# First MLP of a fused attention and two-MLP kernel: the second layer follows the first at a distance of four steps

## The chip, the cores and the metric

The kernel runs on one core of a Trainium2 chip. The metric is the device time of one execution in microseconds; of the kernel before there are three runs, with a median of 1335.04 us (1334.82 to 1335.3). A profile of one more execution (1334.01 us) is what all rows below are read from.

## The reference

Two attention reads per batch and head, joined over 8 batches and 8 heads into 4352 rows (8 batches of 512 tokens and 32 state rows) of width 512, then two MLPs of inner width 2048. Inputs and weights are float64, the result is float32.

```python
scores = scale * x @ state.T;  a = softmax(scores);   xread = a @ state
scores2 = scale * state @ x.T; a2 = softmax(scores2); sread = a2 @ x
x = concat([xread, sread], axis=2) -> (4352, 512)
h = x @ w_in                                            # first MLP
g = where(h >= 1, h, where(h <= -1, 0, (h + 1)**2 / 4))
x = g @ w_out
h = x @ w2_in; g = max(h, 0) + alpha * min(h, 0)        # second MLP
out = g @ w2_out
```

## The kernel before

**Engines.** TensorE (PE) does all products; VectorE (DVE) and ScalarE (ACT) decode weights, drain PSUM, split numbers and apply the activations; SyncE (SP) issues nearly all loads and stores; GpSimd (POOL) issues some small DMAs.

**Number form.** Most products are made of three fast passes: each operand is split into a high part in the short form (`hi_`, on ACT) and a rest (`lo_`, on DVE), and `mm3` or `out_mm` adds three of the four products. A few early products take plain f32 operands instead, which needs no split and more PE time: the first-layer products of steps 0 to 3, the second-layer products of the first `NAT` = 9 steps, and all products that make weights (below).

**The first MLP as steps.** `steps` are 9 x 16 pairs (t, f): t is a block of 512 token columns (t = 0 to 7, one per batch; t = 8 holds the 256 state rows), f one of 16 blocks of 128 of the inner width. For step i three things are done. `h_mm(i)` is the first layer: it fills one PSUM bank with h. `act_fn(i)` turns h into g: two ACT operations into y, then one DVE operation that reads y and the bank, after which the bank is free. `out_mm(i)` is the second layer: it adds w_out[f] times g into four PSUM banks `accA`; after f = 15 `out_end` copies these to SBUF and stores them. From step 9 on g is split by `g_split` one step before its use. Below, h(i), g(i) and out(i) are these three for step i.

**The first layer's weights.** The attention read is folded into w_in: w_in comes in 4 column blocks (blk) of 4 row blocks (c). For each, `vg_mm` multiplies it with the states of a group of four batches, for two groups: two half-height matmuls side by side into two PSUM banks, which ACT copies to `vgo`; SP stores them (`vg_store`), later batches load them back. For batch 0, block 1 is made directly (`vdirect`: two banks `vdp`, split into `vw01..h` and `vw01..l`), and blocks 2 and 3 go from `vgo` by POOL's DMA (`v0_move`) and a split (`vr_hi`, `vr_lo`) into the operands of h(8) and h(12).

**Decoding a weight block.** `d_load` brings 512 KB of float64 (SP). `dec0` takes the high words' absolute value (ACT, line 377); `dec1` does four integer operations (DVE, lines 388, 390, 393, 396). The raw words lie in pool V (14 buffers of 4 KB a partition), nearly all else in pool U (72 buffers of 2 KB). PSUM has two pools of four banks: one for `accA`, one that h, the `vg_mm` pairs and `vdp` share.

**The order of the work.** One loop runs over the steps, and two tables say what else is issued in step i: `side` before `out_mm`, `behind` after it. In step i the program issues h(i+2), then `g_split(i+1)` and the table's entries turn by turn, then `act_fn(i+2)`, then out(i), then `behind`. The framework's planner orders each engine's stream by that order and may move an instruction ahead of one that it takes to be not yet ready; instructions pinned with `keep_in_program_order` are not moved past. Tables before the change: w_in blocks are decoded at steps -3 to 7, the w_out block f at step f-2 (f-3 from f = 9), its load three steps earlier, that of f = 0 ahead of the loop. `vg_mm` runs in the steps -4 to -1 (one each), 1 to 8 (two each, one of them in `behind`), and 9 to 16 (one each).

```python
h_mm(i + 2)
todo.append((act_fn, i + 2))
run(*todo)
out_mm(i)
run(*behind.pop(i, []))
```

The loop ends after step 143; `second()`, the second MLP, follows. Its first operands are prepared at steps 130 to 140 of the loop.

Of the kernel before, what the change touches and what calls it, by code (L numbers as in the profile page):

```python
# [33 lines left out]
NF, NO = FF // 128, DM // 128  # L34
# [6 lines left out]
def kernel_body(ctx: ExitStack, tc: tile.TileContext, x, state, w1i, w1o, w2i, w2o, alpha, out):  # L41
# [10 lines left out]
    def U(name, dt=F32):  # L52
        return up.tile([128, 512], dt, tag="u", name=name)
# [12 lines left out]
    def run(*calls):  # L66


        gens = [g for g in (fn(*a) for fn, *a in calls) if g is not None]
        while gens:  # L70
            gens = [g for g in gens if next(g, gens) is not gens]
# [25 lines left out]
    w2d = dp.tile([8, 7, 128, 512], F32, name="w2d")  # L97
    wd = [dp.tile([DM, 512], F32, name=f"wd{k}") for k in range(4)]
    GRP = [(1, 2, 3, 4), (0, 5, 6, 7)]
    NAT = 9  # L100


    A = {}
# [159 lines left out]
    def sums_out(b, q):  # L263
        a = A[b, q]
        so = small(f"so{b}{q}", 64)
        act.activation(out=so, in_=a.pop("sr"), func=AF.Copy, scale=a.pop("r2"))
        a["so"] = so
# [99 lines left out]
    def d_load(key, src):  # L367
        t = vp.tile([128, 512], U64, tag="v", name="wr_" + "_".join(map(str, key)))
        ld.dma_start(out=t.rearrange("p (k c) -> p k c", k=src.shape[1]) if len(src.shape) > 2 else t, in_=src)
        G["raw", key] = t  # L370


    def dec0(key, on_act=True):
        t = G["raw", key]
        r = G["dec", key] = U("wf_" + "_".join(map(str, key)))
        if on_act:
            act.activation(out=r, in_=t.bitcast(F32).rearrange("p (n t) -> p n t", t=2)[:, :, 1], func=AF.Abs)
        else:
            dve.tensor_scalar(out=r.bitcast(I32), in0=t.bitcast(I32).rearrange("p (n t) -> p n t", t=2)[:, :, 1],
                              scalar1=0x7FFFFFFF, scalar2=None, op0=ALU.bitwise_and)  # L380
# [29 lines left out]
    def decode(key, o):  # L410
        at(o - 1, dec0, key)
        at(o, dec1, key)
# [21 lines left out]
    def wi_load(blk, c):  # L434
        d_load(("wi", blk, c), w1i[c * 128:(c + 1) * 128, blk * 512:(blk + 1) * 512])
# [84 lines left out]
    def src_w1o(f):  # L520
        return w1o[f * 128:(f + 1) * 128, :]
# [18 lines left out]
    steps = [(t, f) for t in range(NB + 1) for f in range(NF)]  # L540

    def gi(t, f):
        return t * NF + f
# [3 lines left out]
    def wd_(t):  # L547
        return 512 if t < NB else 256

    def h_mm(i):  # L550
        t, f = steps[i]
        n = wd_(t)
        blk, c = f // 4, (f % 4) * 128
        fs = slice(c, c + 128)
        ps = PS(f"hA{t}{f}")
        if i < 4:
            for q in range(2):
                pe.matmul(ps, VF[q][:, fs], AT[q], start=(q == 0), stop=(q == 1))
            HP[i] = ps
            return  # L560
        if t < NB:
            terms = []
            for q in range(2):
                vh, vl = VW[t, blk, q]
                ah, al = aT[t, q]
                terms.append((vh[:, fs], vl[:, fs], ah, al))
        else:
            terms = [(W["w1s", blk, k][0][:, fs], W["w1s", blk, k][1][:, fs],
                      XS["h"][:, k * 256:(k + 1) * 256], XS["l"][:, k * 256:(k + 1) * 256]) for k in range(4)]
        mm3(ps[:, :n], terms)  # L570
        HP[i] = ps
# [13 lines left out]
    def g_split(i):  # L585
        n = wd_(steps[i][0])
        g = GG.pop(i)
        if i < NAT:
            GH[i] = g
# [7 lines left out]
    def out_mm(i):  # L597
        t, f = steps[i]
        n = wd_(t)
        if f == 0:  # L600
            for k in range(NO):
                ACC[k] = pa.tile([128, 512], F32, tag="acc", name=f"accA{t}{k}")
        if i < NAT:

            g, w = GH.pop(i), G["dec", ("w1o", f)]
            for k in range(NO):
                pe.matmul(ACC[k], w[:, k * 128:(k + 1) * 128], g, start=(f == 0), stop=(f == NF - 1))  # L607
            return out_end(i)
        gh, gl = GH.pop(i)
        wh, wl = W["w1o", f]  # L610
        for k in range(NO):
            ks = slice(k * 128, (k + 1) * 128)
            prods = ((wh[:, ks], gh[:, :n]), (wh[:, ks], gl[:, :n]), (wl[:, ks], gh[:, :n]))
            for j, (a, b) in enumerate(prods):
                pe.matmul(ACC[k][:, :n], a, b, start=(f == 0 and j == 0), stop=(f == NF - 1 and j == 2))  # L615
        out_end(i)

    def out_end(i):
        t, f = steps[i]
        if f < NF - 1:  # L620
            return
        n = wd_(t)
        for k in range(NO):
            o = U(f"oA{t}{k}")
            if t == 0:
                act.copy(o.rearrange("q (p r) -> q r p", r=4), ACC.pop(k).rearrange("q (r p) -> q r p", r=4))
            elif k % 2:
                dve.tensor_copy(o[:, :n], ACC.pop(k)[:, :n])
            else:
                act.copy(o[:, :n], ACC.pop(k)[:, :n])  # L630
            act.dma_start(out=xd[k, :, t * 512:t * 512 + n], in_=o[:, :n])
# [410 lines left out]
    side = defaultdict(list)  # L1042
# [3 lines left out]
    def at(i, fn, *a):  # L1046
        side[i].append((fn, *a))
# [23 lines left out]
    for b in range(1, NB):  # L1071
        t0 = gi(b - 1, 0)
        for q in range(2):
            o = t0 + (2 if b > 1 else 5)
# [22 lines left out]
        for blk in range(4):  # L1097
            for q in range(2):
                o = t0 + 10 + 4 * blk + q
# [5 lines left out]
    for blk in (1, 2, 3):  # L1105
        for c in range(4):
            o = 4 * blk - 7 + c - (blk > 1)
            if blk > 1 or c > 1:
                at(o - 2, wi_load, blk, c)
            decode(("wi", blk, c), o)  # L1110
    at(1, vdirect, 0, 1)
    for f in range(1, NF):
        o = f - 2 - (f >= NAT)
        if f > 2:
            at(o - 3, d_load, ("w1o", f), src_w1o(f))
        decode(("w1o", f), o)
    for f in range(NF):
        o = gi(1, f - 3) if f < NAT else f - 2
        at(o, dec_hi, ("w1o", f))
        at(o + 1, dec2, ("w1o", f))  # L1120
    for n in range(4):
# [3 lines left out]
    for blk in range(4):  # L1125
        for c in range(4):
            if blk:
                o = 4 * blk - 3 + c
                at(o, vg_mm, 0, blk, c)
                at(o + 2, vg_store, 0, blk, c)  # L1130
                o = 13 + c if blk < 2 else 4 * blk - 7 + c
# [54 lines left out]
        ld_stg(g)  # L1186
    wi_load(0, 2)
    wi_load(0, 3)
    d_load(("w1o", 0), src_w1o(0))
    for n in range(2):  # L1190
        wi_load(1, n)
        d_load(("w1o", n + 1), src_w1o(n + 1))
    for u in range(2):
        ld_x1(1, 0, u)
    wps = PS("warm")
# [30 lines left out]
    vfirst(1)  # L1226
    sums_out(0, 0)
    sums_out(0, 1)
    dec0(("w1o", 0))
    run((sums_turn, 0, 0), (sums_turn, 0, 1), (dec1, ("w1o", 0)))  # L1230
    for i in range(min(side), len(steps)):
        todo = [(g_split, i + 1)] if 0 <= i + 1 < len(steps) else []
        if i in (-4, -3):
            h_mm(i + 4)
            todo.append((act_fn, i + 4))
        todo += side.pop(i, [])
        if 0 <= i < len(steps) - 2:
            h_mm(i + 2)
            todo.append((act_fn, i + 2))
        run(*todo)  # L1240
        if i >= 0:
            out_mm(i)
        run(*behind.pop(i, []))
    second()

# [28 lines left out]
```

## Time and profile before

| | us |
|---|---|
| median of 3 runs | 1335.04 (1334.82 to 1335.3) |
| profiled execution | 1334.01 |
| its span | 1332.2 |
| PE busy | 1324.1 (99%) |
| PE weight loads | 1109.0 (83%) |
| DVE busy | 1026.4 (77%) |
| ACT busy | 765.1 (57%) |
| POOL busy | 187.0 (14%) |

The span is the profile's from the first instruction to the last; the execution's own time is 1.81 us longer. All times in rows are from the span's start. A busy PE is not a PE at its peak: ends of matmuls are modelled, and what counts in a chain of matmuls is the distance from one start to the next.

### The profile page before, as it was taken

The page shows a single profiled execution, that of the slowest core. Times are in us where ns is not written, and L with a number is a line of the kernel's source. Part 1 is how long each engine was busy: PE and PEld are TensorE (multiplying, and loading weights), DVE is VectorE, ACT ScalarE, POOL GpSimd, SP SyncE. Part 2 cuts the span into 40 slices and gives each one's busy share as a digit, 9 for nine tenths or more (in the row PEclk, how much of TensorE's full clock was granted, in tenths as well). Part 3 has the DMA queues.
Part 4 walks back from the last instruction along what each step waited for, and adds up shares of the span by engine and source line. Part 5 has one row for each costly group of instructions (what it writes and reads, how often), then busy time and mean ns, then how long its engine had stood idle before and what let it go on. Part 6 is the DMA issues. An engine that isn't in the chain of part 4 may idle for free.

```text
span 1332.2 us, 21104 instructions
## 1 busy us (share of the span) xinstructions
PE 1324.1 (99%) x6962; PEld 1109.0 (83%) x6962; DVE 1026.4 (77%) x1868; ACT 765.1 (57%) x1502; POOL 187.0 (14%) x284
## 2 busy tenths in 40 slices
PE   9999999999999999999999999999999999999998
PEld 5346688878788888888988888888899999999998
DVE  6988575979697879787868696777868867796875
ACT  5768765666566666676745553544635445562543
POOL 1015400223233322244011000000000000000000
PEclk9999999999999999999999999999999999999999
DMA  9988862654666674576467765866687888869876
GB/s 277 321 302 239 223 141 66 150 181 123 210 152 194 173 235 131 183 245 201 145 211 221 274 206 179 271 202 204 207 278 260 286 266 303 295 224 295 278 252 190
DMA packets 262828, 293.03 MB, mean 220 GB/s; under 512 B 145152, under 2 KB 149824, under 8 KB 262720
## 3 DMA queue, kind: packets, MB, share of 16 engines
q1 hardware_dynamic: 243968, 247.73, 60.2%
q0 software_dynamic: 11904, 34.65, 7.4%
q10 hardware_dynamic: 6848, 9.31, 2.0%
q8 instruction: 56, 0.92, 0.3%
q14 instruction: 52, 0.43, 0.1%
HBM read 224.47 MB, written 66.06 MB: 218 GB/s over the span
## 4 chain that ended last, share of the span: by engine, by line
PE 92%; issue 3%; DVE 2%; ACT 1%; POOL 1%; DMA 1%; SPq 0%; POOLq 0%; DVEq 0%; ACTq 0%
PE accA L615 26%; PE accB L868 25%; PE hB L789 23%; PE hA L85 14%; PE vgp L486 1%; PE accA L607 1%; PE sr L258 1%; POOL vr L497 1%; DMA x<-in_x_dram 0%; PE et L240 0%; PE sc L159 0%; DVE c L815 0%; PE sct L312 0%; PE vdp L144 0%; ACT m L800 0%
## 5 line engine op out<-in xcount | busy, mean ns | idle before, releaser
L868 PE MATMUL accB<-gs,wv 128*128 128x384 f32 (+1 forms) x1668 | 331.4, 357 | 0.0
L868 PEld LDWEIGHTS accB<-gs,wv 128*128 128x128 f32 x1668 | 298.6, 188 | 27.6 <-DVE gs L77 1.9
L789 PE MATMUL hB<-xh,wu 128*128 128x384 f32 (+1 forms) x1120 | 314.6, 357 | 0.1
L789 PEld LDWEIGHTS hB<-xh,wu 128*128 128x128 f32 x1120 | 205.9, 188 | 19.2 <-ACT p L819 1.2
L789 PE MATMUL hB<-xl,wu 128*128 128x384 f32 (+1 forms) x560 | 199.6, 356 | 0.0
L800 ACT ACTIVATE m<-c 128x384 f32<-128x384 f32 (+1 forms) x120 | 68.2, 568 | 141.0 <-DVE c L815 139.5
L583 DVE SCALAR_TENSOR_TENSOR g<-y,hA 128x512 f32<-128x512 f32 (+1 forms) x144 | 93.8, 651 | 52.7 <-ACT y L581 52.1
L802 DVE SCALAR_TENSOR_TENSOR c<-m,beta_sb,c 128x384 f32<-128x384 f32 (+1 forms) x120 | 80.9, 674 | 60.3 <-ACT m L800 56.8
L77 DVE TENSOR_TENSOR gl<-g,gh 128x512 fp32r<-128x512 f32 (+1 forms) x135 | 95.0, 704 | 41.0 <-ACT gh L74 39.7
L580 ACT ACTIVATE y<-hA 128x512 f32<-128x512 f32 (+1 forms) x144 | 82.9, 575 | 69.6 <-PE hA L85 69.4
L77 DVE TENSOR_TENSOR gs<-c,gs 128x384 fp32r<-128x384 f32 (+1 forms) x200 | 113.3, 604 | 6.8 <-ACT gs L850 6.4
L789 PEld LDWEIGHTS hB<-xl,wu 128*128 128x128 f32 x560 | 105.1, 188 | 8.7
L850 ACT CAST gs<-c 128x384 fp32r<-128x384 f32 (+1 forms) x200 | 101.6, 554 | 9.0 <-PE accB L868 8.6
L74 ACT CAST gh<-g 128x512 fp32r<-128x512 f32 (+1 forms) x135 | 80.3, 595 | 45.1 <-DVE g L583 38.5
L581 ACT ACTIVATE y<-y 128x512 f32<-128x512 f32 (+1 forms) x144 | 87.5, 608 | 3.8
L842 DVE TENSOR_TENSOR c<-c,c 128x384 f32<-128x384 f32 (+1 forms) x120 | 71.9, 608 | 2.2
L681 POOL DMA_DIRECT2D w2d<-wo x72 | 50.6, 904 | 132.0 <-DVE wo L77 66.0
L911 ACT COPY o<-accB 128x384 f32<-128x384 f32 (+1 forms) x30 | 15.7, 525 | 79.5 <-PE accB L868 79.4
L815 DVE TENSOR_TENSOR c<-hB,u 128x384 f32<-128x384 f32 (+1 forms) x80 | 48.4, 606 | 13.6 <-PE hB L789 11.7
L77 DVE TENSOR_TENSOR gs<-m,gs 128x384 fp32r<-128x384 f32 (+1 forms) x80 | 46.5, 607 | 12.4 <-ACT gs L850 12.4
L681 POOL DMA_DIRECT2D w1d<-wu x56 | 38.6, 765 | 108.2 <-DVE wu L77 90.6
L489 ACT COPY vgo<-vgp 128x512 f32<-128x512 f32 x64 | 34.3, 591 | 25.5 <-PE vgp L486 24.9
(910 smaller groups left out, 2661.7 us busy)
## 6 DMA issues: line engine op xcount, KB each, us to landing
wu<-w1d SPq DMA_DIRECT2D x280, 256.0 KB
wv<-w2d SPq DMA_DIRECT2D x280, 256.0 KB
vr<-vd SPq DMA_DIRECT2D x56, 256.0 KB
w1d<-wu POOLq DMA_DIRECT2D x56, 256.0 KB, 4.4
w2d<-wo POOLq DMA_DIRECT2D x40, 256.0 KB, 5.4
x<-in_x_dram SPq DMA_DIRECT2D x16, 512.0 KB
wr_wi<-in_moe_w_in_dram SPq DMA_DIRECT2D x16, 512.0 KB
wr_w1o<-in_moe_w_out_dram SPq DMA_DIRECT2D x16, 512.0 KB
```

Of the source, the lines that this page charges most:

```text
L74: act.copy(h, raw)
L77: (eng or dve).tensor_tensor(out=l, in0=raw, in1=h.bitcast(F32), op=ALU.subtract)
L85: pe.matmul(ps, a, b, start=(k == 0), stop=(k == n - 1))
L580: act.activation(out=y[:, :n], in_=ps, func=AF.Relu, bias=0.5, scale=0.5)
L581: act.activation(out=y[:, :n], in_=y[:, :n], func=AF.Square)
L583: dve.scalar_tensor_tensor(out=g[:, :n], in0=y[:, :n], scalar=1.0, in1=ps, op0=ALU.min, op1=ALU.max)
L615: pe.matmul(ACC[k][:, :n], a, b, start=(f == 0 and j == 0), stop=(f == NF - 1 and j == 2))
L681: pool.dma_start(out=dst, in_=src)
L789: pin(pe.matmul(ps, a[:, kk], b, start=(new and m == 0), stop=(m == 5), skip_group_check=True))
L802: dve.scalar_tensor_tensor(out=g, in0=m, scalar=beta_sb[:, f:f + 1], in1=h, op0=ALU.mult, op1=ALU.add)
L850: tc.keep_in_program_order(act.copy(h, src))
L868: pin(pe.matmul(ps, a[:, js], b, start=(new and k == 0 and n == 0), stop=(k == 7 and n == 2), skip_group_check=True))
```

## The change

A constant `LAG` = 4 is added. Out(i) and its `g_split` are issued four steps later, in step i + 4; h(i+2), `act_fn` and all attention and w_in work keep their step. The loop gets four more steps at its end, which hold the last four `out_mm`. The load, the decode and the later split of every w_out block move four steps later too, and block 0, which was loaded and decoded ahead of the loop, goes into the tables like the others. The loads ahead of the loop now bring all four blocks of w_in's column block 1 and none of w_out (before: two of the four, and w_out 0, 1 and 2). Sizes, counts and forms of instructions stay as they are.

```diff
-    NAT = 9
+    NAT, LAG = 9, 4
...
-            if blk > 1 or c > 1:
+            if blk > 1:
                 at(o - 2, wi_load, blk, c)
             decode(("wi", blk, c), o)
     at(1, vdirect, 0, 1)
-    for f in range(1, NF):
-        o = f - 2 - (f >= NAT)
-        if f > 2:
-            at(o - 3, d_load, ("w1o", f), src_w1o(f))
+    for f in range(NF):
+        o = f - 2 - (f >= 9) + LAG
+        at(o - 3, d_load, ("w1o", f), src_w1o(f))
         decode(("w1o", f), o)
     for f in range(NF):
-        o = gi(1, f - 3) if f < NAT else f - 2
+        o = (gi(1, f - 3) if f < NAT else f - 2 + (f < 9)) + LAG
         at(o, dec_hi, ("w1o", f))
         at(o + 1, dec2, ("w1o", f))
...
-    d_load(("w1o", 0), src_w1o(0))
-    for n in range(2):
+    for n in range(4):
         wi_load(1, n)
-        d_load(("w1o", n + 1), src_w1o(n + 1))
...
-    dec0(("w1o", 0))
-    run((sums_turn, 0, 0), (sums_turn, 0, 1), (dec1, ("w1o", 0)))
-    for i in range(min(side), len(steps)):
-        todo = [(g_split, i + 1)] if 0 <= i + 1 < len(steps) else []
+    run((sums_turn, 0, 0), (sums_turn, 0, 1))
+    for i in range(min(side), len(steps) + LAG):
+        todo = [(g_split, i + 1 - LAG)] if 0 <= i + 1 - LAG < len(steps) else []
...
-        if i >= 0:
-            out_mm(i)
+        if i >= LAG:
+            out_mm(i - LAG)
         run(*behind.pop(i, []))
```

## Rows read from the trace of the kernel before

**Rows 1.** The page's first part: busy time, share of the span, instructions.

```profile
PE 1324.1 (99%) x6962; PEld 1109.0 (83%) x6962; DVE 1026.4 (77%) x1868; ACT 765.1 (57%) x1502; POOL 187.0 (14%) x284
```

**Rows 2.** PE's waits, whole span: who for whom, total, times, longest.

```profile
PE vgp L486 <- DVE g L583: 0.8, 1, 0.8
PE hA L85 <- ACT vw031h L74: 0.4, 1, 0.4
```

**Rows 3.** Stretches: length, busy time of each engine, granted clock, DMA share, GB/s.

```profile
29.70:39.80 10.10, 9.23 (x26) 3.13 (x24) 8.59 (x18) 8.51 (x16) 2.37 (x4) 1.00 0.95 332
39.80:71.80 32.00, 32.00 (x103) 12.92 (x102) 30.37 (x63) 21.78 (x40) 4.03 (x6) 1.00 0.97 326
...
200.00:300.00 100.00, 100.00 (x590) 81.05 (x589) 74.12 (x132) 62.03 (x115) 19.23 (x27) 1.00 0.48 133
```

**Rows 4.** PE in order of time, steps -4 to 4: start, duration, instruction.

```profile
29.71 1.98 PE L558 MATMUL hA<-at,vf 128*128 128x512 f32 x4
...
38.77 1.12 PE L486 MATMUL vgp<-wf_wi,sts 64*128 64x512 f32 x2 [0.76 <-DVE g L583]
39.82 1.98 PE L558 MATMUL hA<-at,vf 128*128 128x512 f32 x4
41.64 3.60 PE L607 MATMUL accA<-g,wf_w1o 128*128 128x512 f32 x8
45.07 1.88 PE L558 MATMUL hA<-at,vf 128*128 128x512 f32 x4
...
47.94 1.92 PE L144 MATMUL vdp<-wf_wi,zf 64*32 64x512 f32 x16
49.79 3.70 PE L607 MATMUL accA<-g,wf_w1o 128*128 128x512 f32 x8
53.42 1.13 PE L486 MATMUL vgp<-wf_wi,sts 64*128 64x512 f32 x4
54.48 0.50 PE L85 MATMUL hA<-ath,vw010h 128*128 128x512 f32 x1
...
56.10 1.13 PE L486 MATMUL vgp<-wf_wi,sts 64*128 64x512 f32 x4
...
71.85 3.70 PE L607 MATMUL accA<-g,wf_w1o 128*128 128x512 f32 x8
```

**Rows 5.** ACT in order of time, parts of steps 0, 1 and 3.

```profile
44.30 0.63 ACT L580 ACTIVATE y<-hA 128x512 f32<-128x512 f32 x1
...
49.07 0.59 ACT L74 CAST vw010h<-vdp 128x512 fp32r<-128x512 f32 x1
49.55 0.62 ACT L74 CAST ath<-at 128x512 fp32r<-128x512 f32 x1
...
62.91 0.69 ACT L377 ACTIVATE wf_wi<-wr_wi 128x512 f32<-128x512 f32 x1
63.49 0.67 ACT L377 ACTIVATE wf_w1o<-wr_w1o 128x512 f32<-128x512 f32 x1
64.61 1.07 ACT L489 COPY vgo<-vgp 128x512 f32<-128x512 f32 x2 [0.45 <-PE vgp L486]
65.57 0.61 ACT L580 ACTIVATE y<-hA 128x512 f32<-128x512 f32 x1
66.22 0.63 ACT L581 ACTIVATE y<-y 128x512 f32<-128x512 f32 x1
```

**Rows 6.** DVE in order of time: one g, then the ends of two whole decodes.

```profile
60.42 0.68 DVE L583 SCALAR_TENSOR_TENSOR g<-y,hA 128x512 f32<-128x512 f32 x1
61.02 0.42 DVE L388 TENSOR_SCALAR wf_wi<-wf_wi 128x512 f32<-128x512 f32 x1
...
64.76 0.42 DVE L388 TENSOR_SCALAR wf_wi<-wf_wi 128x512 f32<-128x512 f32 x1
```

**Rows 7.** ACT in order of time: the decode of one w_in block.

```profile
46.18 0.68 ACT L377 ACTIVATE wf_wi<-wr_wi 128x512 f32<-128x512 f32 x1 [0.59 <-DMA wr_wi<-in_moe_w_in_dram]
```

**Rows 8.** The chain that ended last, in order of time: one split second-layer step.

```profile
116.73 2.97 PE accA L615 x12
```

## The prediction

> **What bounds the kernel now.** I read the page's first part, then PE's waits, then stretches, then PE, ACT and DVE in order of time around steps -4 to 4. PE is busy for 1324.1 of 1332.2 us [rows 1], and 100.00 of 100 us in the first MLP's long run [rows 3]: in all that follows the opening there is nothing to win. PE's waits behind the first few microseconds are few; two matter here, 0.8 us before a `vg_mm` matmul that wanted a PSUM bank which g(1) had still to free, and 0.4 us in h(12), whose operand came late through POOL's DMA [rows 2]. In the opening the other engines are as full as PE: in 29.7 to 39.8 DVE is busy for 8.59 and ACT for 8.51 of 10.10 us, in 39.8 to 71.8 DVE for 30.37 of 32.00, at a DMA share of 0.95 and 0.97 [rows 3]. So the opening decides, and the question is whether PE still has enough to do there when four second-layer steps leave it.
>
> **What is moved, not changed.** No instruction is added or removed; steps 0 to 8 keep the plain f32 form. The sum of PE's work stays, and the time changes only by PE's idle time. From h(2) to the first `out_mm` PE's work is, from start to start in rows 4: h(2) 1.82 (39.82 to 41.64); h(3) with a `vg_mm` 2.87 (45.07 to 47.94); `vdirect` 1.85 (47.94 to 49.79); one more `vg_mm` 1.06 (53.42 to 54.48), 7.60 for steps 0 and 1. Steps 2 and 3: h 1.62 (54.48 to 56.10) and two `vg_mm`, 3.74 each. Step 4: h and one `vg_mm`, 2.68. Together 17.76. The other way round: 39.82 to 71.85 is 32.03, less out(0) 3.43 (41.64 to 45.07) and three outs of 3.63 (49.79 to 53.42), 17.71. Without waits out(0) would start at 57.5 and all behind it would stand as before.
>
> **ACT in that stretch.** Its prices [rows 5]: a decode's first operation 0.58 (62.91 to 63.49), the two copies of a `vg_mm` 0.96 (64.61 to 65.57), y 1.28 (65.57 to the end of the second at 66.85), a cast 0.48 (49.07 to 49.55). A step without `out_mm` wants two decodes, two pairs of copies and one y: 4.36 us, against PE's 3.74. ACT falls behind by 0.62 in each of steps 2 and 3. In step 1 it has more. y(2) began at 44.30 [rows 5] and ended 1.28 later; three w_out decodes ahead of it go (1.74), so it ends at about 43.8. Then come two decodes, a pair of copies, two casts and y(3), 4.36, to 48.2, and g(3) on DVE, 0.60 (60.42 to 61.02) [rows 6], to 48.8. Only then is h(3)'s bank free for h(4), since the other three hold the `vdp` pair, whose split still reads them, and a `vg_mm`. PE is there at 39.82 + 7.60 = 47.4: 1.4 late. Before, out(1) with its 3.63 lay over this chain; that cover is gone. Sum for PE: 1.4 + 2 x 0.62 = 2.6.
>
> **DVE.** A decode costs (64.76 - 61.02) / 2 = 1.87 [rows 6]. With a `lo_` or a transpose priced as g, steps 0 to 3 want 4.94 (two decodes), 4.27, 5.54 and 4.34, 19.1 in all, from 39.8 to about 59. PE needs of this g(5), and one decoded w_out block, so DVE leads to the same 60 or so and adds nothing to ACT's 2.6.
>
> **DMA.** In 39.8 to 71.8 it moved 326 GB/s x 32 us = 10.4 MB at a share of 0.97. Four w_out blocks less (2.1 MB) leaves 8.3 MB wanted in 17.7 + 2.6 us, 410 GB/s, more than the 326 and 332 of these rows. Most of it are stores that nobody waits for soon, and one raw block less lies in V ahead of the loop (11 loads instead of 12), so that w_in loads can start earlier than before. ACT did wait once for a w_in block, 0.59 [rows 7]. I put half of that, 0.3, on the path; bounds: below, -0.6 (that wait goes); above, 2 us, from the rival on late data.
>
> **Given back.** h(12)'s wait of 0.4, with slower matmuls on either side 0.5: in step 9 PE now has a plain out (3.63) where it had a split one (2.97) [rows 4, 8], 0.7 more cover for the same chain. -0.5. The waits of steps -4 to -1 stay: g(0) and g(1) are behind ACT's y there, not behind DVE's w_out decode. If they went, it would be up to 2.2 more (the faster rival).
>
> **Edits at nothing.** The decode, load and split of each w_out block keep their distance to out(f), and the decodes of step 9 on move beside emptier DVE steps. Four more g tiles lie in U: counted in the program's order before has at most 67 of 72 alive (step 12), where the change holds nine w_out tiles less; later at most 64. PSUM's `accA` banks are copied out four steps later, beside the next batch's softmax; DVE has 26 and ACT 38 us of 100 free there [rows 3], and h(i+2) runs between the last use and the next. If a copy (0.6, as a PSUM read in rows 5) were late each time, 0.6 x 8 = 4.8. The four outs at the loop's end have inputs ready and weights in SBUF; `second()`'s operands are issued at the same steps, now earlier against PE. SP loses one load ahead of the loop, POOL nothing.
>
> **Sum.** 2.6 + 0.3 - 0.5 = +2.4. In the profiled execution's time 1334.01 becomes 1336.4; the runs' median stands 1.03 above it, so 1337.4.
>
> **The rivals.**
>
> Slower by the opening's own rate. From 29.71 to 39.82, the stretch that already lacks second-layer work, PE had h(0), h(1) (1.82 each) and four `vg_mm` (1.06), 7.88, and took 10.11: 28% more. The mechanism is the four shared banks: when the second matmul of a pair waits for a bank, it runs alone, and alone it takes 1.05 (38.77 to 39.82), as long as both side by side [rows 4]. At 28% the 17.7 us lose 5.0; less the 0.5 given back +4.5, 1339.5. It decides from a loss of 3.2 on. For it: the same five tiles a step over four banks. Against it: ACT there waited for PE, and carried w_out decodes too. PE's granted clock was 1.00 in the stretch with the 0.76 us of waiting [rows 3, 4], the upper level (2.4 GHz), and the f32 h behind the wait takes 1.98 like the one ahead of it. The Trainium skill (TensorE: Matmul & The Clock Gate, "Part 1: The HAM clock gate") says that idleness brings the half clock back; the trace shows none here, and by the rule the first out behind a wait would cost 3.4 us more.
>
> Late data. A w_in block, or POOL's DMA for h(8), lands behind the crowd of stores: 1 to 2 us more than the forecast, about 1339. For: share 0.97; against: SP gets room in V earlier.
>
> Covered. The planner fills PE's gaps with out(0), whose inputs are ready from step 2 on, or moves ACT's early decodes into ACT's gaps in steps -4 to -1: loss near 0.5, net 0 to +1, 1335.5. For: the planner may order so. Against: in the 0.76 us ahead of 38.77 PE waited, nothing was moved up, and out(0) came in its own place at 41.64 [rows 4].
>
> Faster. The waits of steps -4 to -1 (2.2) go with the w_out decodes, nothing new comes: -2.7, 1332.3. What remains of PE's idle time is ahead of this. The Trainium skill (Perfetto Trace Analysis, "Identifying the Most-Contended Engine") holds weight loads, not matmul time, for the measure of PE's headroom; by it 39.8 to 71.8 at 12.92 of 32.00 against 81.05 of 100.00 [rows 3] would have 16 us to give. The rows disagree: eight f32 matmuls in 3.63 us start 0.45 apart without a gap [rows 4]; a weight load is short beside such a matmul, so that its low share says nothing of room.
>
> **Chances and range.** Forecast 0.42 (net +1.2 to +3.2), slower by the rate 0.27, late data 0.10, covered 0.15, faster 0.06. 0.2% is 2.7 us, about what a measurement of this kernel tells from no change. The upper fifth of the forecast's case (0.08) lies above it: slower 0.45, same 0.49, faster 0.06. The range leaves out the faster case and the top of the slower ones: 1334.6 to 1341.0; the forecast's own is 1336.2 to 1338.2.
>
> **What would show it.** First out at about 60 (57.5 would be covered, 62.5 the rate). h(4) waiting for g(3) or for the `vdp` split; ACT without gaps from 40 to 58; in h(12) no wait. Behind step 16 PE's times unchanged but for a shift. Wrong would be: an idle PE anywhere behind step 16, waits of more than 3.2 us before the first out, or a shorter stretch -4 to -1.

## The result, and the profile after

The kernel after takes 1342.13 us (median of 6 runs, 1340.88 to 1344.76) against 1334.68 us (6 runs, 1333.57 to 1335.3) of the kernel before beside it: a ratio of 1.0058, 95% interval 1.0045 to 1.0071, or 7.45 us slower. The forecast was 1337.4, or 2.4 slower, and its range ended at 1341.0: the direction is right, the size is three times that of the forecast. The profiled execution took 1341.26 us, its span is 1339.2, 7.0 longer than before.

The page's first part of the kernel after, against [rows 1]:

```profile
PE 1329.3 (99%) x6962; PEld 1110.5 (83%) x6962; DVE 1021.8 (76%) x1868; ACT 759.0 (57%) x1502; POOL 188.0 (14%) x284
```

The same 6962 PE instructions are busy for 5.2 us more, so of the 7.0 us only 1.8 are idle time. PE's waits over the whole span, against [rows 2] (who for whom, total, times, longest):

```profile
PE vgp L486 <- DVE g L583: 2.1, 2, 1.3
PE warm L1194 <- DVE warm L1176: 1.5, 1, 1.5
PE sc L144 <- ACT xt L300: 0.9, 1, 0.9
```

The wait of a `vg_mm` for g grew from 0.8 to 2.1, that of h(12) is gone, the others are of the first microseconds. What grew in busy time is one group. By line, operation and tile: busy time, mean ns of one, idle time before. After:

```profile
L486 PE MATMUL vgp<-wf_wi,sts 64*128 64x512 f32 x128 | 42.3, 635 | 2.2 <-DVE g L583 2.1
```

Before:

```profile
L486 PE MATMUL vgp<-wf_wi,sts 64*128 64x512 f32 x128 | 37.5, 638 | 0.9 <-DVE g L583 0.8
```

128 records with the same mean duration each cover 4.8 us more. They can, because before most of them ran two at a time: what a reader must look at is not the duration of one but how far one start is from the next. Summed from start to start without idle time, the group went from 35.5 to 40.5 us (+5.0), and PE's idle time from 2.35 to 4.18 (+1.8). That is 6.8 of the 7.0. The rest is small items that nearly cancel: the score matmuls at 153 us +1.0, the warm-up's length -0.5, and switches between the two number forms, which seem to fall on the first layer where they fell on the second (+1.4 and -1.6).

PE in order of time after the change, against [rows 4] (start, duration, instruction; x4 is a whole `vg_mm` pair, x2 one half of it):

```profile
39.78 3.70 PE L558 MATMUL hA<-at,vf 128*128 128x512 f32 x8
43.41 1.13 PE L486 MATMUL vgp<-wf_wi,sts 64*128 64x512 f32 x4
44.60 1.96 PE L144 MATMUL vdp<-wf_wi,zf 64*32 64x512 f32 x16
46.49 1.12 PE L486 MATMUL vgp<-wf_wi,sts 64*128 64x512 f32 x2
48.95 1.12 PE L486 MATMUL vgp<-wf_wi,sts 64*128 64x512 f32 x2 [1.34 <-DVE g L583]
50.00 0.50 PE L85 MATMUL hA<-ath,vw010h 128*128 128x512 f32 x1
...
51.59 2.92 PE L486 MATMUL vgp<-wf_wi,sts 64*128 64x512 f32 x8
...
56.02 1.98 PE L486 MATMUL vgp<-wf_wi,sts 64*128 64x512 f32 x6
57.94 7.13 PE L607 MATMUL accA<-g,wf_w1o 128*128 128x512 f32 x16
...
65.00 1.12 PE L486 MATMUL vgp<-wf_wi,sts 64*128 64x512 f32 x2
...
67.64 2.92 PE L486 MATMUL vgp<-wf_wi,sts 64*128 64x512 f32 x8
...
79.81 1.12 PE L486 MATMUL vgp<-wf_wi,sts 64*128 64x512 f32 x2
...
81.29 1.12 PE L486 MATMUL vgp<-wf_wi,sts 64*128 64x512 f32 x2
...
84.26 1.13 PE L486 MATMUL vgp<-wf_wi,sts 64*128 64x512 f32 x4
```

Three things are to be seen. The pair of step 1 is torn: its first half runs at 46.49, its second waits 1.34 for g(3)'s bank and runs alone from 48.95 to 50.00. Two pairs in a row (51.59) take 2.85 from start to start where two whole ones take 2 x 1.06 = 2.12. And at 56.02 one half goes with the pair ahead of it, out(0) and out(1) are put behind it, and the pair's other half follows alone at 65.00. Such halves go on until 82.34; from 84.26 on pairs are whole, as all of them are in [rows 4] from 53.42 on.

The stretches, against [rows 3] (length, busy time of PE, PE's loads, DVE, ACT, POOL, granted clock, DMA share, GB/s):

```profile
29.70:39.80 10.10, 9.27 (x27) 3.12 (x25) 6.82 (x13) 7.98 (x15) 1.80 (x4) 1.00 0.86 292
39.80:71.80 32.00, 30.60 (x97) 12.71 (x97) 28.36 (x57) 22.62 (x43) 3.26 (x6) 1.00 1.02 342
200.00:300.00 100.00, 100.00 (x591) 81.28 (x590) 71.86 (x130) 60.40 (x115) 19.78 (x27) 1.00 0.43 123
```

DVE lost 1.77 us of work in 29.70 to 39.80 and h(2) still began at 39.78 (before 39.82). In the long run nothing changed. Where nothing but h and out stands between, out(i) of the changed kernel starts 12.07 us behind that of before, in out(22) to out(25) and again in out(35) to out(41). That is four h of 1.36 (5.44) and a loss of 6.63: nearly all of the loss lies ahead of out(18), at 172.6 us.

### The profile page after: what moved, and what is told of

Its sections match the earlier page's. It is cut to its first block, busy times and chain, and to the rows that moved or that the text cites. A ratio compares the mean times of both kernels' runs of the same rounds, so it can differ in the third digit from the quotient of the medians.

```text
span 1339.2 us, 21228 instructions
## 1 busy us (share of the span) xinstructions
PE 1329.3 (99%) x6962; PEld 1110.5 (83%) x6962; DVE 1021.8 (76%) x1868; ACT 759.0 (57%) x1502; POOL 188.0 (14%) x284
## 4 chain that ended last, share of the span: by engine, by line
PE 95%; DVE 2%; ACT 1%; DMA 0%; issue 0%; SPq 0%; ACTq 0%; DVEq 0%
PE accA L615 26%; PE accB L868 24%; PE hB L789 23%; PE hA L85 14%; PE accA L607 2%; PE vgp L486 2%; PE sc L159 1%; PE sr L258 1%; DMA x<-in_x_dram 0%; PE et L240 0%; DVE c L815 0%; PE sct L312 0%; ACT m L800 0%; PE hA L558 0%; DVE wf_wi L393 0%
## 5 line engine op out<-in xcount | busy, mean ns | idle before, releaser
L77 DVE TENSOR_TENSOR gl<-g,gh 128x512 fp32r<-128x512 f32 (+1 forms) x135 | 92.3, 686 | 27.4 <-ACT gh L74 25.9
```

The lines of the kernel that those rows point to most:

```text
L77: (eng or dve).tensor_tensor(out=l, in0=raw, in1=h.bitcast(F32), op=ALU.subtract)
```

## The experiments

Each kernel was timed in 3 rounds beside the kernel before, which took 1334.04 (19 runs), 1334.30 (13) and 1334.22 us (13) in the three sets: e1 to e4, e5 to e8, e9 to e11. The theories: the banks (B): half a pair that runs alone costs as much as a pair, and, without an `out_mm` in each step, PE comes to the four shared banks too early. The planner's order (P): it, not the banks, tears pairs apart. The moved decodes (D). The opening's rate (R): ACT and DVE set the pace, whatever PE does.

**e1: what a torn pair costs.** In the kernel before, the eight pairs of steps 9 to 16 are taken apart, the first half ahead of `out_mm`, the second behind it. No work is added.

```diff
...
-                at(o, vg_mm, 0, blk, c)
+                at(o, vg_mm, 0, blk, c, (0,) if blk == 3 else (0, 1))
+                if blk == 3:
+                    by(o, vg_mm, 0, blk, c, (1,))
...
-                by(o, vg_mm, 1, blk, c)
+                if blk == 1:
+                    at(o, vg_mm, 1, blk, c, (0,))
+                by(o, vg_mm, 1, blk, c, (1,) if blk == 1 else (0, 1))
```

> The kernel before, with eight of its vg_mm pairs (block 3 of the first group, block 1 of the second, steps 9 to 16) taken apart: the first half-height matmul stays ahead of out_mm, the second goes behind it. No work is added. It prices the loss: theory A (a half alone takes PE as long as the pair, 1.05 us against 1.06) expects 8 x 1.05 = +8.4 us, 1343. The rival (a half alone costs half of a pair, and the longer vgp time in the changed kernel is only how waits are shown) expects no change, 1334.7 within 1 us.

Measured: 1343.38 us, ratio 1.0069 (1.0054 to 1.0084), 9.3 slower. The group, and one torn pair of the trace:

```profile
L486 PE MATMUL vgp<-wf_wi,sts 64*128 64x512 f32 x128 | 46.4, 638 | 0.9 <-DVE g L583 0.8
```

```profile
109.69 1.12 PE L486 MATMUL vgp<-wf_wi,sts 64*128 64x512 f32 x2
110.75 0.50 PE L615 MATMUL accA<-gh,w_w1o_9h 128*128 128x512 f32 x1
...
113.71 1.12 PE L486 MATMUL vgp<-wf_wi,sts 64*128 64x512 f32 x2
114.76 0.50 PE L85 MATMUL hA<-ath,vw030h 128*128 128x512 f32 x1
```

Each half alone holds PE for 1.06 and 1.05, the whole pair for 1.06 [rows 4]; from start to start the group grew by 8.4, PE's idle time not at all. So tearing eight pairs costs 8.4 us that no view of waits shows. The Trainium skill (TensorE: Matmul & The Clock Gate, "Why this matters for your kernels") says that a matmul with few rows takes as long alone as a full one and gains only beside others. This trace agrees: one half alone takes 1.05, two side by side 1.06, and a full-height f32 matmul of the same width 0.91 ([rows 4], 1.82 for the two of h(2)).

**e2: the planner's hand taken off.** The kernel after, with PE's matmuls of steps -4 to 12 pinned to program order.

```diff
+    def pin0(ins):
+        if G.get("pin", False):
+            tc.keep_in_program_order(ins)
...
-            pe.matmul(ps[u], ST[g][rows, c * 128:(c + 1) * 128], w[rows], start=True, stop=True)
+            pin0(pe.matmul(ps[u], ST[g][rows, c * 128:(c + 1) * 128], w[rows], start=True, stop=True))
...
+        G["pin"] = i < 13
```

> The changed kernel with PE's first- and second-layer, vg_mm and vdirect matmuls of steps -4 to 12 held in the program's order, so that no second-layer matmul can be put between the halves of a pair. Theory P (the planner's own reordering splits the pairs, three of them for about 3 us, and takes cover from later steps) expects 1338 to 1339, 3 to 4 us off the change's 1342.1. Theory B (the banks make PE wait whatever the order) expects the lone halves to come back as waits ahead of the first out, at 60 or later, and 1341 to 1343. Theory R (ACT and DVE are simply too slow for the steps without out_mm) expects the same 1341 to 1343.

Measured: 1340.30, ratio 1.0044 (1.0029 to 1.0059), between the bands of P and of B. It is 1.8 under after, but the two intervals overlap, so that a gain isn't shown. With out(0) back in its place, at 65.11, the group still takes 40.2 us from start to start, about 1 of it at half the clock (last section), and the waits are longer (after 2.1); one of them, 0.85, stands just ahead of the first out, as B had it. The order is a small part at most.

```profile
L490 PE MATMUL vgp<-wf_wi,sts 64*128 64x512 f32 x128 | 42.0, 653 | 3.0 <-DVE g L587 3.0
```

**e3: other banks.** The kernel after, with the early pairs (through step 3) in the four `accA` banks, which stand idle until the first out.

```diff
-        ps = [(PS if blk or c > 1 else acc_ps)(f"vgp{g}{blk}{2 * c + u}") for u in range(2)]
+        early = blk == 0 or (c < 3 and (g, blk) in ((0, 1), (1, 2)))
+        ps = [(acc_ps if early else PS)(f"vgp{g}{blk}{2 * c + u}") for u in range(2)]
```

> The changed kernel, where the vg_mm pairs of steps -4 to 3 take their PSUM banks from the four of accA, which lie idle until the first out_mm; h and vdp keep the other four. Theory B (bank shortage) expects nearly all of the loss to go, 1335 to 1337. Theory R (ACT and DVE rate) expects little, 1340 to 1342: PE then runs ahead and waits for the first decoded blocks instead. Theory P expects 1339 to 1341, as the planner still moves some second-layer matmuls.

Measured: 1335.93, ratio 1.0015 (1.0006 to 1.0025): 1.9 above before, where after was 7.45 above. The banks are the cause of some 5.6 us of the loss. The `vg_mm` group is back at 35.4 us from start to start:

```profile
L487 PE MATMUL vgp<-wf_wi,sts 64*128 64x512 f32 x128 | 37.2, 634 | 0.0
```

The opening in order of time:

```profile
37.93 3.70 PE L559 MATMUL hA<-at,vf 128*128 128x512 f32 x8
41.56 1.13 PE L487 MATMUL vgp<-wf_wi,sts 64*128 64x512 f32 x4
42.62 1.91 PE L144 MATMUL vdp<-wf_wi,zf 64*32 64x512 f32 x12
45.25 1.05 PE L144 MATMUL vdp<-wf_wi,zf 64*32 64x512 f32 x4 [0.72 <-DVE wf_wi L396]
46.23 1.13 PE L487 MATMUL vgp<-wf_wi,sts 64*128 64x512 f32 x4
47.29 0.50 PE L85 MATMUL hA<-ath,vw010h 128*128 128x512 f32 x1
...
49.60 0.50 PE L85 MATMUL hA<-ath,vw010l 128*128 128x512 f32 x1 [0.53 <-DVE vw010l L77]
...
58.12 1.13 PE L487 MATMUL vgp<-wf_wi,sts 64*128 64x512 f32 x4
59.18 4.56 PE L608 MATMUL accA<-g,wf_w1o 128*128 128x512 f32 x10
...
67.13 1.09 PE L159 MATMUL sc<-xt,sts 64*32 64x512 f32 x16 [0.74 <-DVE g L584]
```

h(2) begins 1.85 earlier, and no `vg_mm` waits. What is left of the span is 1.7 us: idle time is 0.8 above before and `vdp` 1.1. `vdirect` is at a decoded block too early (0.72), so that its last quarter runs apart and the whole takes 2.89 from start to start without the wait, where it took 1.85; h(4) is at the split of `vdp` too early (0.53), and the score matmuls at a g (0.74). The Trainium skill's advice to use all eight banks (Perfetto Trace Analysis, "Matmul Optimizations") holds here, with 5.6 us back, and not in the next kernel.

**e4: the same banks in the kernel before**, for the pairs of steps -4 to -1.

```diff
-        ps = [(PS if blk or c > 1 else acc_ps)(f"vgp{g}{blk}{2 * c + u}") for u in range(2)]
+        ps = [(PS if blk else acc_ps)(f"vgp{g}{blk}{2 * c + u}") for u in range(2)]
```

> The kernel before, where the vg_mm pairs of steps -4 to -1 take accA's idle banks. The changed kernel's step -4 to -1 has the same 2.2 us lost as the kernel before. Theory B expects 1.5 to 2.5 us less than before, about 1332.7; theory R expects no change, 1334.7 within 0.5.

Measured: 1334.19, ratio 1.0002 (0.9992 to 1.0011): a miss. h(2) came 1.8 us earlier (38.01), but PE then stood before the next things that ACT and DVE had not yet done (the wait of h(12) grew from 0.4 to 0.6):

```profile
PE accA L607 <- ACT vgo L489: 0.7, 1, 0.7
PE hA L85 <- ACT vw031h L74: 0.6, 1, 0.6
PE hA L85 <- DVE vw011l L77: 0.3, 1, 0.3
```

The first of these is a bank again: out(0) stands before two `accA` banks that ACT has not yet drained of a pair. R's forecast, no change, came true: PE was 1.8 us ahead and gained nothing, since it waited elsewhere for what ACT and DVE had still to do.

**e5: the distance without the moved decodes.** The kernel before, only out and `g_split` four steps later; w_out is loaded and decoded as before.

```diff
...
-        o = gi(1, f - 3) if f < NAT else f - 2
+        o = (gi(1, f - 3) if f < NAT else f - 2) + LAG
...
-        if i >= 0:
-            out_mm(i)
+        if i >= LAG:
+            out_mm(i - LAG)
```

> The kernel before with the second layer alone four steps later: all w_out loads and decodes stay where they were (the later split into high and low parts moves along). It tells the distance apart from the deferred decodes. Theory B (banks) expects the same kind of loss, since the pairs of steps -4 to 3 still share four banks: 1339 to 1344. If the deferred loads and decodes were the cause (theory D), it would come out at 1334 to 1336. Theory R (ACT and DVE rate) expects more than the change, 1343 to 1347, as w_out's decodes are back in the steps without out_mm.

Measured: 1342.86, ratio 1.0064 (1.0048 to 1.0081), as slow as after, with an even longer group (42.9 from start to start). Theory D falls: the distance alone does it. The time is in B's band, and R's, 1343 to 1347, begins 0.14 above it: this run doesn't part those two, e3 does.

```profile
L486 PE MATMUL vgp<-wf_wi,sts 64*128 64x512 f32 x128 | 44.7, 633 | 1.4 <-DVE g L583 0.8 <-ACT vgo L489 0.5
```

**e6: half the distance** (`LAG` 2).

> The changed kernel with a distance of two steps in place of four: the steps without out_mm are -4 to 1 instead of -4 to 3. Theory B: the loss of 7 comes from lone halves and waits in and just behind the steps 1 to 3, where two pairs and an h share four banks, so that two of three such steps go: +2 to +4, 1336 to 1338. A loss that grows as the number of steps (7.4 x 2/4) gives +3.7; a loss of the order at large, not of the distance, +6 to +7.

Measured: 1342.79 (1340.35 to 1345.79), ratio 1.0062 (1.0043 to 1.0082): a miss for both forecasts that let the loss shrink with the distance; the median is 8.5 above before, and the two runs at the fuller clock (last section) 6.1 and 6.7, the +6 to +7 of "the order at large". Torn pairs cost less (the group is 39.1), idle time more (6.7, after 4.2), a part of it far behind the opening, at 439 us:

```profile
PE vdp L144 <- ACT vgo L489: 1.4, 1, 1.4
PE vdp L144 <- DVE g L583: 1.3, 1, 1.3
PE hA L85 <- ACT so L266: 1.1, 1, 1.1
```

**e7: DVE emptied.** e3 without DVE's decode of w_out 0 to 3.

```diff
+        if key[0] == "w1o" and key[1] < 4:
+            return
```

> The changed kernel with accA's idle banks for the early vg_mm pairs, and besides the four DVE operations of the decode of w_out blocks 0 to 3 left out (those blocks hold only the high words' absolute value; 7.5 us of DVE work less in steps 2 to 5). It asks what the 1.9 us are that remain with the banks. If DVE's fullness sets them (theory R for the rest), 1333 to 1334.5; if they are the vdirect chain of step 1 and 2, which has no out_mm over it any more and lies ahead of these decodes, 1335.5 to 1336.5.

Measured: 1335.51, ratio 1.0010 (1.0001 to 1.0020), 1.2 above its own before, where e3 was 1.9 above; the two intervals overlap. The waits of `vdp` and h(4) are as in e3, and `vdp` is as long. The 0.74 of the score matmuls is gone: DVE's fullness is at most that part of what is left.

**e8: a distance of one, with the banks of e4.**

> A distance of one step, with accA's idle banks for the vg_mm pairs of steps -4 to -1. Out(0) then stands behind vdirect in step 1 and covers the split of its two banks, and one step only has no out_mm beyond before's. Theory B with the vdirect chain expects 1332.5 to 1334.5, at or under the kernel before (1334.0 to 1334.7). If DVE is what holds PE in steps -1 to 4 whatever the order, 1334.5 to 1336.

Measured: 1343.35 (1341.07 to 1347.1), ratio 1.0068 (1.0046 to 1.0090): a miss, 9 us above B's band and 7 above the other. The group is 38.1 from start to start, +2.6; PE's idle time is 1.6 more, `vdp` 1.0, the score matmuls 1.9. A reading that e9 tests: the planner now has a ready second-layer product for every half that must wait. Between 51.15 and 54.31 two halves of a pair, 1.06 and 1.05 alone, have an `accA` product between them.

**e9: e8 pinned** as in e2.

> Distance of one step instead of four, the vg_mm pairs of steps -4 to -1 in accA's idle banks as in e8_lag1_banks, and PE's matmuls of steps -4 to 12 held in the order in which the program issues them. Theory 'the planner's order': e8 was slow (1343.35) because the planner put second-layer matmuls between the halves of pairs; held together, no half runs alone before step 13, the vg_mm group falls from 38.1 to about 35.5-36 us and the time to 1334.5-1337. Theory 'banks alone': a half waits for its bank whatever the order, PE stands idle where the planner had put an accA matmul, the vg_mm group or PE's idle time stays 2 us or more above before, 1339-1343.

Measured: 1340.47, ratio 1.0045 (1.0030 to 1.0060). The group is whole again (34.7 from start to start), but the time is in the band of "banks alone", which expected either the group or PE's idle time to stay 2 us above before: idle time is 3.1 above. PE now stands idle where the planner had put an `accA` product.

```profile
41.34 1.13 PE L490 MATMUL vgp<-wf_wi,sts 64*128 64x512 f32 x4
46.24 1.06 PE L148 MATMUL vdp<-wf_wi,zf 64*32 64x512 f32 x8 [3.77 <-DVE g L587]
47.56 2.40 PE L148 MATMUL vdp<-wf_wi,zf 64*32 64x512 f32 x8 [0.26 <-ACT vgo L493]
```

A torn pair and a wait are two faces of one lack, a bank that isn't free. The score matmuls take 1.5 more than before here too. The slow `vdp` (2.40) and the out behind it ran partly at half the clock (last section).

**e10: a distance of two, with other banks** for the pairs of steps -4 to 1.

> Distance of two steps with accA's idle banks for the early vg_mm pairs of steps -4 to 1 (as in e3_banks, as far as the distance lets them be idle). Theory 'banks': the opening's part of the loss goes, 1334.5-1337.5 (e6_lag2 was 1342.8). Theory 'the order at large' (each distance gives the planner another order for the whole kernel, with its own losses): the opening's part goes but waits and lone halves appear elsewhere, as in e8; 1339-1343.

Measured: 1340.12, ratio 1.0048 (1.0033 to 1.0063): 2.7 under e6 by the medians and 1.4 between the two profiled executions (1339.56 and 1340.98), with intervals that overlap. Most of the loss stays, in the band of "the order at large": the group is 2.2 above before, the wait behind 430 us is there (at 437), and `vdp` waits 2.0 for its decoded block.

**e11: e3 pinned.**

> e3_banks (distance four, early pairs in accA's idle banks) with PE's matmuls of steps -4 to 12 held in program order. Theory 'vdirect chain': what was left in e3 (+1.9 us) is h(4) and vdp waiting for ACT's splits, which no order of PE shortens: 1335.5-1337, the same waits. Theory 'planner': the rest is its order, and the time falls to 1333.5-1335.

Measured: 1336.54, ratio 1.0021 (1.0011 to 1.0031), no better than e3. The program's order doesn't shorten the `vdirect` chain either; held in it, h(4) waits longer for the split:

```profile
PE hA L89 <- DVE vw010l L81: 1.6, 1, 1.6
```

No kernel was faster than before.

## Why the prediction was wrong

**The step that failed** is the sentence "The sum of PE's work stays, and the time changes only by PE's idle time." Instructions and forms stayed, their sum didn't. It priced idle time alone, +2.4, and idle time rose by 1.8. Beside it the `vg_mm` group grew by 5.0 without one more instruction, because 17.76 and the 1.06 in it hold only while both halves of a pair have a bank. What a torn pair costs e1 shows; that the banks tear it, e3.

**The rival had the mechanism.** "Slower by the opening's own rate" said that the second half of a pair, when it waits for a bank, runs alone and takes 1.05. It got 0.27 and 1339.5, since the 28% were laid on the 17.7 us ahead of out(0). The halves went on to 82.34, far past out(0): the distance leaves PE with products ready to put between them. The argument against it, "ACT there waited for PE, and carried w_out decodes too", didn't speak against it: after the change ACT waits for PE too, 1.05 before it can copy the half that ran late (at 50.11), and e5, with all those decodes, is not clear of after (intervals 1.0048 to 1.0081 and 1.0045 to 1.0071).

**ACT's chain at h(4)** came out nearly to the letter. It forecast g(3) done at 48.8, PE there at 47.4. ACT after the change, the two operations of y(3) [rows 5]:

```profile
46.79 0.64 ACT L580 ACTIVATE y<-hA 128x512 f32<-128x512 f32 x1
47.46 0.63 ACT L581 ACTIVATE y<-y 128x512 f32<-128x512 f32 x1
```

And DVE, which ends the chain [rows 6]:

```profile
47.61 0.68 DVE L77 TENSOR_TENSOR atl<-at,ath 128x512 fp32r<-128x512 f32 x1
48.22 0.68 DVE L583 SCALAR_TENSOR_TENSOR g<-y,hA 128x512 f32<-128x512 f32 x1
48.81 0.68 DVE L77 TENSOR_TENSOR vw010l<-vdp,vw010h 128x512 fp32r<-128x512 f32 x1
```

g(3) ends at 48.90 and PE waited 1.34 from 47.61. But the bank that came free went to the pair's second half, alone, so h(4) began at 50.00 and not at 48.8. "DVE adds nothing" was near the edge: from 40 to 48.9 it ran with no gap over 0.2, and y(3) was ready at 48.09, only 0.13 ahead of g(3)'s start. In the profile's chain that ended last, 37.99 to 48.90 is DVE's alone. So the time of the chain was right, and in part by luck: another engine was full just as long. The 2 x 0.62 of steps 2 and 3 did not come as waits: there is no idle PE between 50 and 84, only torn pairs.

**Smaller terms.** DMA +0.3: nothing came; ACT has no wait for a w_in block in 36 to 84, where it had 0.59 [rows 7]. h(12)'s wait, -0.5: it went, 0.4. The waits of steps -4 to -1 stayed (0.76 ahead of 38.73), as said. The faster rival falls with that, and e4 shows besides that nothing was to be had there. "Covered" was half right in a way that helped nobody: the planner does pull out(0) and out(1) forward, which the prediction held against it, and puts them between two halves.

**The signs.** "First out at about 60 (57.5 would be covered, 62.5 the rate)" was a bad sign to choose: it came at 57.94 with the whole loss on its way, because the planner had moved it ahead of half a pair; held in order (e2) it came at 65.11, some 1.5 of it from the clock. "Waits of more than 3.2 us before the first out" was no better, since the loss is in busy time. "Behind step 16 unchanged" held, but for 1.0 us in the score matmuls, whose 16 records took twice their usual 1.0 in the chain that ended last; why is open:

```profile
153.61 2.00 PE sc L159 x16
```

**What stays open.** The last 1.9 us of e3 were read as the `vdirect` chain, which lost out(1)'s cover; e7 takes at most 0.7 of it away with DVE's load, e11 nothing with PE's order, and no run made that chain shorter. The losses at distances one and two are located in part (at `vdp`: a bank in e6, e8 and e9, a decoded block in e10; the score matmuls; waits at 160 to 440 us in e6 and e10), not removed. That the planner's order causes those behind the opening isn't shown.

## What to carry to other kernels

Work that is moved away from a step doesn't only leave idle time: it may have been the pause in which shared PSUM banks came free, and its going can break up matmuls that share PE side by side, which the profile counts as busy. Before a product is moved, ask which tiles are packed, what each half waits for, and what the planner will put between them. And a sum of work is compared start to start by tile, not by waits or by the duration of one instruction.

## What was not expected of the hardware

In the opening the clock fell in three of the twelve profiles with changes, each time behind one of the opening's waits: in e2 (1.35 us of waiting from 47.67), e9 (3.77) and e11 (1.6). These are the three kernels with pinned matmuls. In e2, by stretches:

```profile
45.00:50.90 5.90, 4.55 (x24) 1.42 (x17) 5.90 (x13) 4.80 (x11) 0.51 (x1) 1.00 0.83 242
50.90:54.40 3.50, 3.50 (x9) 1.73 (x8) 3.50 (x8) 1.06 (x3) 0.51 (x1) 0.51 1.16 269
54.40:60.00 5.60, 5.60 (x18) 2.33 (x17) 4.33 (x10) 5.48 (x11) 1.22 (x2) 1.00 1.00 336
```

3.5 us at 0.51 of full speed, the lower level (1.2 GHz), cost about 1.5 us, while PE itself was busy all through: from h(4) to the end of h(5) the same work took 7.57 (from 50.07), where the kernel after took 6.02 (from 50.00). The kernel after, with the same wait of 1.34, kept 1.00 in its profile, and so did e6 with two waits of 1.3 and 1.4 and e10 with one of 2.0: a wait of that length doesn't settle it.

It differs from run to run of one kernel. The granted clock, as the mean of a whole run, was 1.000 in the two runs of e8 at 1341.07 and 1341.13 us, and 0.998 and 0.996 in those at 1345.58 and 1347.10; in e6 it was 0.999 at 1340.35 and 1340.98, and 0.997 at 1344.60 and 1345.79. So the spread of 5 to 6 us in these two, where the kernel before spreads by 2 to 2.5, goes with the clock, and their medians stand about 2 us above their runs with the higher clock. Where in those runs it fell isn't on record. The Trainium skill's rule on idleness, which the prediction weighed (TensorE: Matmul & The Clock Gate, "Part 1: The HAM clock gate"), is thus borne out in some profiles and not in others, at less than half the 3.4 us that the prediction put beside it.
